# Fewer, wider loads of the factor rows on two queues, and three batches of attention in turns

## The chip, the cores and the metric

One Trainium2 chip, one core. The metric is the device time of one execution in microseconds (us); lower is better. The kernel before takes 1417.87 us (median of 3 runs, 1416.62 to 1419.35).

## What is computed

Eight batches, each of 8 heads, 576 tokens and 64 values a head, all in float32. `phi` gives each head 32 memory slots: a softmax over the tokens weighs keys and values into 32 rows each, and every token attends to these rows. The result, a row of 512 per token, goes through a "mixture of depths": a gate scores every token, the 128 best of a batch pass a two-layer network, and the others keep their row.

```python
a = softmax(phi, over tokens)            # (b, h, 576, 32)
k_m, v_m = a^T k, a^T v                  # (b, h, 32, 64)
x = softmax(q k_m^T / 8) v_m             # (b, 576, 8 * 64)
top = the 128 best of x w_gate, in each batch
out = x;  out[top] = x[top] + sigmoid(x[top] w_gate) * (relu(x[top] w1) w2)
```

## The kernel before, in words

The program is written out by hand: every engine and every DMA queue works off its instructions in the order in which the Python code issues them. Jobs are generators; `turns` (L580) steps up to `width` of them round-robin and starts a new one at least `lag` rounds after the last, `beside` (L594) puts `n` steps of another job behind each step of the first.

**Softmax and splitting (stage A, groups 0 to 7; stage B, groups 8 to 15).** A group is half a batch (4 heads). `softmax` (L156) is long work of VectorE (DVE) with ScalarE (ACT) beside it, and two groups are in turns with lag 6. Its tail `keys` (L269) transposes the weights on TensorE (PE), splits them into a high and a low part (`ahi`, `alo`, L282 to L284) and stores eight pieces to the scratch `aparts` in HBM from the queue of GpSimd (POOL, L288); another piece of `keys` forms `k_m` (L294). Beside stage A, `split_v` (L250) loads each half batch of `v` into one of two buffers (`vb`, SP queue, L254), splits it on DVE (L256, L258) and stores four copies to `vparts` from POOL (L262).

**The sums `v_m` (`values`, L303).** One call does four batches at once: `values(0)` beside stage B, `values(1)` beside the attention of batches 0 to 3 (stage C), each with two steps behind every step of the main job (L616, L633). The 576 tokens are cut into 16 chunks of T = 36. `load` (L310) brings a chunk into one of two pairs of buffers (`v_rows`, `a_rows`) by 16 transfers, all on the SP queue: eight of `a_rows` (L314; 16 partitions eight apart, pieces of 128 B, 72 KB) and then eight of `v_rows` (L320; 16 neighbouring partitions, 9216 B each, 144 KB). The loads of chunk `ch + 1` are issued as chunk `ch` begins, into the buffers that chunk `ch - 1` has left. PE then does 4 matmuls a token (L334), 2304 in all; every 16 of them are one step, so `values` has 144 steps.

**Attention and network (stage C, batches 0 to 3; stage D, batches 4 to 7).** A batch is one generator (`attention_and_ffn`, L561) of 37 steps: `centre` (L345; its first PE instruction is L348), then for three thirds of the tokens `scores` (L395) and `attend` (L435), where a third goes PE (L403), DVE (L408, L410), ACT (L412, L413), DVE (L415), PE (L443), ACT (L445), PE (L451), DVE (L454), POOL (two adds, L458), DVE (`score`, L428 to L433) and to HBM (L461); then `rank` (L465; DVE, L485, L487), `gather` (L494), `ffn1` (L514; PE L537) and `ffn2` (L544; PE L550, DVE L554, and the scatter on POOL, L556). Two batches are in turns with lag 10. All PE results pass through four PSUM banks used in turn (`bank`, L84); `xj` has two buffers, `qb`, `es` and `rd` four.

Of the kernel before, what the change touches and what calls it, by code (L numbers as in the profile page):

```python
# [9 lines left out]
F32 = mybir.dt.float32  # L10
# [5 lines left out]
AF = mybir.ActivationFunctionType  # L16
# [4 lines left out]
P = 128  # L21
# [17 lines left out]
def kernel(  # L39
# [26 lines left out]
    SET = 4  # L66
    T = 36
    scale = 1.0 / Dh ** 0.5
# [15 lines left out]
    def bank(shape, dtype=F32):  # L84
        return pss.tile(list(shape), dtype, tag="bank", name="bank")
# [11 lines left out]
    def load_q(b, j):  # L97
        qs[b, j] = step.tile([P, NPR, 2 * PT], F32, name="qb", bufs=4)
        nc.sync.dma_start(out=qs[b, j], in_=qT[b, j])
# [8 lines left out]
    kbd = [const.tile([P, NPR, 2 * M], F32, name=f"kbd{i}") for i in range(B)]  # L108
    vbd = [const.tile([P, 2, NPR * Dh], F32, name=f"vbd{i}") for i in range(2)]

# [139 lines left out]
    def split_v(b):  # L250

        for u in range(2):
            vb = io.tile([P, S * Dh * NPR // P], F32, name="vb")
            nc.sync.dma_start(out=vb, in_=v[b, u])  # L254
            hi = io.tile([P, S * Dh * NPR // P], F32, name="vhi")
            nc.vector.tensor_single_scalar(hi.bitcast(I32), vb.bitcast(I32), -4096,  # L256
                                           op=ALU.bitwise_and)
            nc.vector.tensor_sub(vb, vb, hi)  # L258
            yield
            for vp, src in enumerate((vb, hi)):  # L260
                for ap in range(2):
                    nc.gpsimd.dma_start(  # L262
                        out=vparts[b, u, ap, vp].rearrange("r s d -> (r s d)")
                                                .rearrange("(p x) -> p x", p=P), in_=src)
            yield
# [3 lines left out]
    def keys(b, g):  # L269
# [15 lines left out]
        for h in range(4):  # L285
            r, u = 2 * g + h // 2, h % 2
            for part, src in enumerate((lo, hi)):
                nc.gpsimd.dma_start(  # L288
                    out=aparts[r, b, u, part].rearrange("(c p) m -> p c m", p=PT),
                    in_=src[:, :, h * M:(h + 1) * M])  # L290
        km = bank([P, 2, 2 * M])
        for rr in range(2):
# [10 lines left out]
    def values(st):  # L303
# [6 lines left out]
        def load(ch):  # L310
            ss = slice(ch * T, (ch + 1) * T)
            for vp in range(2):
                for r in range(NPR):
                    nc.sync.dma_start(  # L314
                        out=a_rows[ch % 2][vp * 4 + r::8, :, r].bitcast(F32),
                        in_=aparts[r, b0:b0 + SET].rearrange("b u t s m -> (b u t) s m")[:, ss])
            for bb in range(SET):
                for u in range(2):
                    p0 = bb * 32 + u * 16
                    nc.sync.dma_start(  # L320
                        out=v_rows[ch % 2][p0:p0 + 16, u].rearrange("p s d -> p (s d)").bitcast(F32),
                        in_=vparts[b0 + bb, u].rearrange("t w r s d -> (t w r) (s d)")
                            [:, ch * T * Dh:(ch + 1) * T * Dh])

# [20 lines left out]
    def centre(b):  # L345
# [32 lines left out]
        for r in range(NPR):  # L378
            rows = slice(r * M, (r + 1) * M)
            nc.scalar.activation(vbd[b % 2][rows, :, r * Dh:(r + 1) * Dh], tp[rows], AF.Copy)  # L380
        means = []
# [13 lines left out]
    def scores(b, j):  # L395
# [5 lines left out]
        for c in range(2):  # L401
            for r in range(NPR):
# [7 lines left out]
        nc.vector.tensor_sub(d, heads, mx.unsqueeze(2).to_broadcast([PT, 2 * H, M]))  # L410
        e = step.tile([PT, 2 * H, M], F32, name="es", bufs=4)
        nc.scalar.activation(e, d, AF.Exp, scale=scale)  # L412
# [3 lines left out]
                                       op0=ALU.add, op1=ALU.mult)  # L416
        rd = step.tile([PT, 2, 2, NPR], F32, name="rd", bufs=4)
        rd_f = rd.rearrange("p c u r -> p (c u r)")
# [16 lines left out]
    def attend(b, j):  # L435
# [12 lines left out]
        for c in range(2):  # L448
            o = bank([PT, 2, NPR, Dh])
            for u in range(2):  # L450
                nc.tensor.matmul(out=o[:, u].rearrange("p r d -> p (r d)"), lhsT=eT[:, c, u],  # L451
                                 rhs=vbd[b % 2][:, u], start=True, stop=True)
            yield
            nc.vector.tensor_mul(x[:, c].rearrange("p (r u d) -> p u r d", u=2, d=Dh), o,  # L454
                                 rd[:, c].unsqueeze(3).to_broadcast([PT, 2, NPR, Dh]))
# [120 lines left out]
    def finish(job):  # L576
        for _ in job:
            pass
# [15 lines left out]
    def beside(main, other, n):  # L594

        for _ in main:
            for _ in range(n):
                next(other, None)
            yield
# [19 lines left out]

    work = ctx.enter_context(tc.tile_pool(name="work", bufs=2))  # L620
    one = ctx.enter_context(tc.tile_pool(name="one", bufs=1))
# [6 lines left out]
    def batch(b):  # L628
        load_q(b, 0)
        yield from attention_and_ffn(b)  # L630

    sums = values(1)
    finish(beside(turns([batch(b) for b in range(SET)], 10), sums, 2))  # L633
    finish(sums)
    finish(turns([batch(b) for b in range(SET, B)], 10))

# [33 lines left out]
```

## Time and profile before

| | |
|---|---|
| median of 3 runs | 1417.87 us |
| profiled execution: its time | 1417.34 us |
| its span (first to last instruction) | 1415.6 us |
[...]
| busy share of the span | DVE 62%, PE 51%, POOL 21%, ACT 19% |

The profile is of one execution. Times are counted from the first instruction. A share of busy time is a mean over four stages with different limits, so the stages are looked at one by one: the prediction reads windows of the span, the chain of work that ended last in a stage, the waits of an engine, and single instructions in order of time. "SPq" is the queue of SP, which issues DMAs; the share of DMA is the mean over 16 DMA engines of the time that packets took, and can pass 1 where packets overlap.

### The profile page before, as it was taken

The numbers are of one execution on the slowest core, as the hardware profiler recorded it, in microseconds if no ns is written. First come the engines' busy times: TensorE is split into PE (matmuls) and PEld (weight loads), VectorE is DVE, ScalarE is ACT, GpSimd is POOL, SyncE is SP. The second block draws the span as 40 slices with busy tenths as digits, with TensorE's granted clock in tenths as the row PEclk, the third lists the DMA queues.
The fourth block names the chain that finished last, engine by engine and source line by source line (L and its number), as shares of the span: only waits on it lengthen the run. The fifth ranks groups of instructions, "written<-read, shape, count | busy, mean of one in ns | idle before, by whom it ended". The sixth has DMA issues, their size and how long they took to land.

```text
span 1415.6 us, 16937 instructions
## 1 busy us (share of the span) xinstructions
PE 724.6 (51%) x6656; PEld 617.9 (44%) x6656; DVE 874.7 (62%) x1480; ACT 272.4 (19%) x489; POOL 297.8 (21%) x312
## 2 busy tenths in 40 slices
PE   0011111112377767842168998978545662675265
PEld 0011111112366757741157776857434542554254
DVE  8989999997857997878103234223573267346731
ACT  2212233332323332322001100002200120012000
POOL 7143211112011110111101131100431024103420
PEclk9999999999999999999999999978757755678567
DMA  6798811112999898930788888781110111010100
GB/s 195 299 360 310 336 42 42 42 42 46 122 159 144 140 152 145 154 57 17 191 129 126 142 143 138 119 151 38 56 52 19 38 56 42 22 38 30 33 19 23
DMA packets 190718, 156.05 MB, mean 110 GB/s; under 512 B 160560, under 2 KB 162608, under 8 KB 186544
## 3 DMA queue, kind: packets, MB, share of 16 engines
q1 hardware_dynamic: 171312, 94.15, 37.1%
q0 software_dynamic: 19328, 60.83, 13.4%
q8 instruction: 53, 0.87, 0.3%
q14 instruction: 25, 0.20, 0.1%
HBM read 96.21 MB, written 58.72 MB: 109 GB/s over the span
## 4 chain that ended last, share of the span: by engine, by line
DVE 34%; PE 24%; DMA 14%; SPq 12%; POOL 8%; issue 4%; ACT 3%; DVEq 0%; POOLq 0%; ACTq 0%
DMA v_rows<-vparts 9%; SPq L314 8%; PE acc L334 8%; POOL xj L458 7%; PE bank L537 5%; PE bank L550 3%; SPq L320 3%; PE bank L451 2%; PE bank L294 2%; DVE low L194 2%; DVE lo L190 2%; DVE low L193 2%; PE bank L503 2%; DVE big L191 2%; DVE lo L192 2%
## 5 line engine op out<-in xcount | busy, mean ns | idle before, releaser
L334 PE MATMUL acc<-v_rows,a_rows 32*128 32x128 f32 x4608 | 286.5, 409 | 143.0 <-DMA v_rows<-vparts 132.6
L334 PEld LDWEIGHTS acc<-v_rows,a_rows 32*128 32x128 f32 x4608 | 264.6, 319 | 172.9 <-issue 136.3
L276 PE MATMUL bank<-ident,e 128*96 128x128 f32 x96 | 24.0, 423 | 327.7 <-DVE e L245 327.7
L458 POOL TENSOR_TENSOR xj<-xj,mean 96x1024 f32<-96x1024 f32 x48 | 118.7, 2476 | 308.7 <-DVE xj L454 229.4
L276 PEld LDWEIGHTS bank<-ident,e 128*96 128x96 f32 x96 | 16.7, 193 | 330.5 <-issue 286.1
L288 POOL DMA_DIRECT2D aparts<-alo x64 | 47.1, 736 | 444.1 <-DVE alo L284 444.1
L451 PE MATMUL bank<-vbd,eT 128*96 128x256 f32 x192 | 82.4, 597 | 40.9 <-ACT eT L445 40.9
L294 PE MATMUL bank<-aS,kb 96*128 96x64 f32 x384 | 86.1, 423 | 11.7 <-ACT aS L278 11.7
L294 PEld LDWEIGHTS bank<-aS,kb 96*128 96x128 f32 x384 | 83.1, 331 | 16.5 <-ACT aS L278 15.8
L428 DVE TENSOR_TENSOR prod<-xj,wg 96x1024 f32<-96x1024 f32 x24 | 37.8, 1576 | 68.0 <-POOL xj L458 68.0
L537 PE MATMUL bank<-xeT,w_sb 128*128 128x128 f32 x512 | 73.1, 314 | 7.0 <-ACT xeT L531 7.0
L537 PEld LDWEIGHTS bank<-xeT,w_sb 128*128 128x128 f32 x512 | 71.4, 229 | 10.1 <-ACT xeT L531 10.0
L451 PEld LDWEIGHTS bank<-vbd,eT 128*96 128x96 f32 x192 | 45.8, 256 | 61.9 <-ACT eT L445 43.4
L554 DVE SCALAR_TENSOR_TENSOR ye<-bank,gr,xe 128x512 f32<-128x512 f32 x8 | 6.0, 751 | 105.0 <-PE bank L550 105.0
L408 DVE TENSOR_REDUCE smx<-bank 96x16 f32<-96x512 f32 x24 | 16.2, 673 | 87.4 <-PE bank L403 87.4
L454 DVE TENSOR_TENSOR xj<-bank,rd 96x512 f32<-96x512 f32 x48 | 31.7, 675 | 56.2 <-PE bank L451 56.2
L403 PE MATMUL bank<-kbd,qb 128*96 128x64 f32 x384 | 57.2, 332 | 8.9 <-DMA qb<-in_qT 8.9
L403 PEld LDWEIGHTS bank<-kbd,qb 128*96 128x96 f32 x384 | 56.1, 247 | 10.7 <-issue 9.1
L190 DVE SCALAR_TENSOR_TENSOR lo<-num,vh 128x576 f32<-128x576 f32 x48 | 36.2, 754 | 37.0 <-ACT vh L151 37.0
L550 PE MATMUL bank<-w_sb,hT 128*128 128x512 f32 x128 | 56.5, 594 | 0.0
L503 PE MATMUL bank<-tok,pick 96*128 96x1 f32 x96 | 21.6, 352 | 59.4 <-DVE pick L498 59.4
L194 DVE TENSOR_TENSOR low<-low,lo 128x576 f32<-128x576 f32 x64 | 48.5, 758 | 2.2
(129 smaller groups left out, 1307.7 us busy)
## 6 DMA issues: line engine op xcount, KB each, us to landing
v_rows<-vparts SPq DMA_DIRECT2D x256, 144.0 KB, 6.0
vparts<-vb POOLq DMA_DIRECT2D x32, 576.0 KB, 5.7
vparts<-vhi POOLq DMA_DIRECT2D x32, 576.0 KB, 7.5
a_rows<-aparts SPq DMA_DIRECT2D x256, 72.0 KB, 3.8
kb<-in_k SPq DMA_DIRECT2D x16, 576.0 KB, 7.8
vb<-in_v SPq DMA_DIRECT2D x16, 576.0 KB, 6.1
qb<-in_qT SPq DMA_DIRECT2D x24, 384.0 KB, 3.8
out<-xj POOLq DMA_DIRECT2D x24, 384.0 KB, 3.3
```

The lines of the kernel that those rows point to most:

```text
L190: stt(out=lo, in0=val, scalar=GRID, in1=h, op0=ALU.mult, op1=ALU.subtract)
L194: tt(out=low, in0=low, in1=lo, op=ALU.add)
L288: nc.gpsimd.dma_start(out=aparts[r, b, u, part].rearrange("(c p) m -> p c m", p=PT), in_=src[:, :, h * M:(h + 1) * M])
L294: nc.tensor.matmul(out=km[:, rr], lhsT=kb[:, c, rr * P:(rr + 1) * P], rhs=aS[:, c, rr * 2 * M:(rr + 1) * 2 * M], start=(c == 0), stop=(c = ...
L314: nc.sync.dma_start(out=a_rows[ch % 2][vp * 4 + r::8, :, r].bitcast(F32), in_=aparts[r, b0:b0 + SET].rearrange("b u t s m -> (b u t) s m") ...
L334: nc.tensor.matmul(out=accs[bb][:, :P].rearrange("p (u d) -> p u d", d=Dh), lhsT=ar[p, s].rearrange("p r m -> p (r m)"), rhs=vr[p, :, s], ...
L403: nc.tensor.matmul(out=sc[:, c, :, r], lhsT=qb[:, r, c * PT:(c + 1) * PT], rhs=kbd[b][:, r], start=True, stop=True)
L451: nc.tensor.matmul(out=o[:, u].rearrange("p r d -> p (r d)"), lhsT=eT[:, c, u], rhs=vbd[b % 2][:, u], start=True, stop=True)
L458: nc.gpsimd.tensor_add(x, x, t.unsqueeze(1).to_broadcast([PT, 2, D]))
L503: nc.tensor.matmul(out=ps[:n], lhsT=pick[:, c, :n], rhs=tok[:, c:c + 1], start=(c == 0), stop=(c == NC - 1))
L537: nc.tensor.matmul(out=ps[:, f, :n], lhsT=w1_sb[:, d, (f0 + f) * P:(f0 + f + 1) * P], rhs=xeT[:, d, :n], start=(d == 0), stop=(d == KD - 1))
L550: nc.tensor.matmul(out=ps[:n], lhsT=hT[:, f, :n], rhs=w2_sb[:, f], start=(f == 0), stop=(f == KF - 1))
```

## The change

Five things change together. (1) The chunk is 32 tokens instead of 36, so 18 chunks instead of 16. (2) `vparts` has its halves `u` outermost, so that a chunk of `v_rows` comes by two transfers of 64 partitions (every second one, 8192 B each) instead of eight. (3) `aparts` holds each part twice: POOL stores the eight pieces of a group as before, and then two new DMAs from HBM to HBM write the second copy of the low and of the high parts; the eight transfers of a chunk of `a_rows` have the same shape as before but for T, and go four each to the SP queue and to the POOL queue, behind the two of `v_rows`. (4) Three batches are in turns instead of two, in both stages, with the buffers that go with it (`vbd`, `work` three instead of two; `qb`, `es`, `rd` six instead of four). (5) In stage C one step of `values(1)` follows each step of the batches, instead of two.

```diff
--- before.py
+++ after.py
@@ -64,7 +64,7 @@
     F = w1.shape[1]
     KD, KF = D // P, F // P
     SET = 4
-    T = 36
+    T = 32
     scale = 1.0 / Dh ** 0.5
     out_flat = out.rearrange("b s d -> (b s) d")
 
@@ -95,7 +95,7 @@
         nc.sync.dma_start(out=ks[b, g], in_=k[b, g])
 
     def load_q(b, j):
-        qs[b, j] = step.tile([P, NPR, 2 * PT], F32, name="qb", bufs=4)
+        qs[b, j] = step.tile([P, NPR, 2 * PT], F32, name="qb", bufs=6)
         nc.sync.dma_start(out=qs[b, j], in_=qT[b, j])
 
     groups = [(b, g) for b in range(B) for g in range(NG)]
@@ -106,7 +106,7 @@
     make_identity(nc, ident)
 
     kbd = [const.tile([P, NPR, 2 * M], F32, name=f"kbd{i}") for i in range(B)]
-    vbd = [const.tile([P, 2, NPR * Dh], F32, name=f"vbd{i}") for i in range(2)]
+    vbd = [const.tile([P, 2, NPR * Dh], F32, name=f"vbd{i}") for i in range(3)]
 
 
     v_rows = [rows.tile([P, 2, T, Dh], F32R, name=f"v_rows{i}") for i in range(2)]
@@ -260,7 +260,7 @@
             for vp, src in enumerate((vb, hi)):
                 for ap in range(2):
                     nc.gpsimd.dma_start(
-                        out=vparts[b, u, ap, vp].rearrange("r s d -> (r s d)")
+                        out=vparts[u, b, ap, vp].rearrange("r s d -> (r s d)")
                                                 .rearrange("(p x) -> p x", p=P), in_=src)
             yield
 
@@ -286,8 +286,12 @@
             r, u = 2 * g + h // 2, h % 2
             for part, src in enumerate((lo, hi)):
                 nc.gpsimd.dma_start(
-                    out=aparts[r, b, u, part].rearrange("(c p) m -> p c m", p=PT),
+                    out=aparts[r, u, b, part, 0].rearrange("(c p) m -> p c m", p=PT),
                     in_=src[:, :, h * M:(h + 1) * M])
+        for part in range(2):
+            copies = aparts[2 * g:2 * g + 2].rearrange("r u b t w s m -> b t w (r u) (s m)")[b, part]
+            copies = copies.rearrange("w h (x y) -> w x h y", x=16)
+            nc.gpsimd.dma_start(out=copies[1], in_=copies[0])
         km = bank([P, 2, 2 * M])
         for rr in range(2):
             for c in range(NC):
@@ -309,18 +313,16 @@
 
         def load(ch):
             ss = slice(ch * T, (ch + 1) * T)
-            for vp in range(2):
-                for r in range(NPR):
-                    nc.sync.dma_start(
-                        out=a_rows[ch % 2][vp * 4 + r::8, :, r].bitcast(F32),
-                        in_=aparts[r, b0:b0 + SET].rearrange("b u t s m -> (b u t) s m")[:, ss])
-            for bb in range(SET):
+            for u in range(2):
+                nc.sync.dma_start(
+                    out=v_rows[ch % 2][u::2, u].rearrange("p s d -> p (s d)").bitcast(F32),
+                    in_=vparts[u, b0:b0 + SET].rearrange("b t w r s d -> (b t w r) (s d)")
+                        [:, ch * T * Dh:(ch + 1) * T * Dh])
+            for r in range(NPR):
                 for u in range(2):
-                    p0 = bb * 32 + u * 16
-                    nc.sync.dma_start(
-                        out=v_rows[ch % 2][p0:p0 + 16, u].rearrange("p s d -> p (s d)").bitcast(F32),
-                        in_=vparts[b0 + bb, u].rearrange("t w r s d -> (t w r) (s d)")
-                            [:, ch * T * Dh:(ch + 1) * T * Dh])
+                    (nc.sync, nc.gpsimd)[u].dma_start(
+                        out=a_rows[ch % 2][2 * r + u::8, :, r].bitcast(F32),
+                        in_=aparts[r, u, b0:b0 + SET].rearrange("b t w s m -> (b t w) s m")[:, ss])
 
         n = S // T
         load(0)
@@ -377,7 +379,7 @@
                             in_=vl.rearrange("p r m -> p (r m)"), identity=ident)
         for r in range(NPR):
             rows = slice(r * M, (r + 1) * M)
-            nc.scalar.activation(vbd[b % 2][rows, :, r * Dh:(r + 1) * Dh], tp[rows], AF.Copy)
+            nc.scalar.activation(vbd[b % 3][rows, :, r * Dh:(r + 1) * Dh], tp[rows], AF.Copy)
         means = []
         for i, src in enumerate((hi, lo)):
             yield
@@ -408,13 +410,13 @@
         nc.vector.tensor_reduce(mx, heads, axis=AX.X, op=ALU.max)
         d = step.tile([PT, 2 * H, M], F32, name="d")
         nc.vector.tensor_sub(d, heads, mx.unsqueeze(2).to_broadcast([PT, 2 * H, M]))
-        e = step.tile([PT, 2 * H, M], F32, name="es", bufs=4)
+        e = step.tile([PT, 2 * H, M], F32, name="es", bufs=6)
         nc.scalar.activation(e, d, AF.Exp, scale=scale)
         nc.scalar.activation(d, d, AF.Tanh, scale=scale / 2)
         yield
         nc.vector.scalar_tensor_tensor(out=e, in0=e, scalar=1.0, in1=d,
                                        op0=ALU.add, op1=ALU.mult)
-        rd = step.tile([PT, 2, 2, NPR], F32, name="rd", bufs=4)
+        rd = step.tile([PT, 2, 2, NPR], F32, name="rd", bufs=6)
         rd_f = rd.rearrange("p c u r -> p (c u r)")
         nc.vector.tensor_reduce(rd_f, e, axis=AX.X, op=ALU.add)
         nc.vector.tensor_scalar(out=rd_f, in0=rd_f, scalar1=float(M), scalar2=1e-9,
@@ -449,7 +451,7 @@
             o = bank([PT, 2, NPR, Dh])
             for u in range(2):
                 nc.tensor.matmul(out=o[:, u].rearrange("p r d -> p (r d)"), lhsT=eT[:, c, u],
-                                 rhs=vbd[b % 2][:, u], start=True, stop=True)
+                                 rhs=vbd[b % 3][:, u], start=True, stop=True)
             yield
             nc.vector.tensor_mul(x[:, c].rearrange("p (r u d) -> p u r d", u=2, d=Dh), o,
                                  rd[:, c].unsqueeze(3).to_broadcast([PT, 2, NPR, Dh]))
@@ -617,7 +619,7 @@
     finish(sums)
     first.close()
 
-    work = ctx.enter_context(tc.tile_pool(name="work", bufs=2))
+    work = ctx.enter_context(tc.tile_pool(name="work", bufs=3))
     one = ctx.enter_context(tc.tile_pool(name="one", bufs=1))
     step = ctx.enter_context(tc.tile_pool(name="step", bufs=2))
     w1_sb = one.tile([P, KD, F], F32, name="w1_sb")
@@ -630,9 +632,9 @@
         yield from attention_and_ffn(b)
 
     sums = values(1)
-    finish(beside(turns([batch(b) for b in range(SET)], 10), sums, 2))
+    finish(beside(turns([batch(b) for b in range(SET)], 10, 3), sums, 1))
     finish(sums)
-    finish(turns([batch(b) for b in range(SET, B)], 10))
+    finish(turns([batch(b) for b in range(SET, B)], 10, 3))
 
 
 def kernel(q, k, v, phi, moe_w_gate, moe_w1, moe_w2, moe_capacity):
@@ -661,8 +663,8 @@
         args.append(nc.dram_tensor(f"in_{name}", a.shape, mybir.dt.from_np(a.dtype),
                                    kind="ExternalInput").ap())
     out = nc.dram_tensor("out", (B, S, H * Dh), F32, kind="ExternalOutput").ap()
-    vparts = nc.dram_tensor("vparts", (B, 2, 2, 2, H // 2, S, Dh), F32, kind="Internal").ap()
-    aparts = nc.dram_tensor("aparts", (H // 2, B, 2, 2, S, phi.shape[3]), F32, kind="Internal").ap()
+    vparts = nc.dram_tensor("vparts", (2, B, 2, 2, H // 2, S, Dh), F32, kind="Internal").ap()
+    aparts = nc.dram_tensor("aparts", (H // 2, 2, B, 2, 2, S, phi.shape[3]), F32, kind="Internal").ap()
     with tile.TileContext(nc) as tc:
         tile_abc_attention__then__mixture_of_depths_kernel(tc, *args, out, vparts, aparts, int(moe_capacity))
     r = run_bass_kernel_spmd(nc, [arrays], core_ids=[0])
```

## Rows read from the trace of the kernel before

**Rows 1.** Windows (start:end, length; PE, PEld, DVE, ACT, POOL busy; PE clock; DMA share; GB/s).

```profile
213.00:320.00 107.00, 20.37 (x90) 18.68 (x90) 97.40 (x154) 35.10 (x57) 17.07 (x24) 1.00 0.16 42
363.00:613.00 250.00, 174.72 (x2367) 162.73 (x2367) 202.91 (x317) 73.11 (x116) 34.77 (x48) 1.00 0.98 146
681.00:1119.00 438.00, 308.66 (x3087) 256.49 (x3088) 150.13 (x310) 41.49 (x91) 73.57 (x44) 0.88 0.57 105
711.00:962.00 251.00, 213.02 (x2598) 181.96 (x2602) 75.31 (x155) 20.14 (x44) 35.95 (x21) 0.95 0.80 133
1142.49:1281.55 139.06, 80.41 (x394) 63.25 (x394) 75.23 (x158) 20.34 (x45) 36.96 (x22) 0.68 0.14 42
1378.00:1412.00 34.00, 19.60 (x97) 14.97 (x96) 9.12 (x21) 1.88 (x4) 3.04 (x3) 0.75 0.05 16
```

**Rows 2.** Chain of waits that ended last, by line, 363 to 613 us.

```profile
by line: DMA v_rows<-vparts 32.6%; SPq L314 28.3%; PE acc L334 14.3%; SPq L320 12.5%; PE bank L294 8.7%; issue 2.6%; PE bank L276 1.2%
```

**Rows 3.** Waits of PE, 363 to 613 us: total, times, longest.

```profile
PE acc L334 <- DMA v_rows<-vparts: 78.1, 43, 13.6
```

**Rows 4.** Waits of DVE, 363 to 613 us.

```profile
DVE lo L190 <- ACT vh L151: 20.7, 13, 6.3
DVE ahi L282 <- ACT aS L278: 16.1, 3, 9.5
```

**Rows 5.** Timeline of the SP queue, 567 to 599 us: start, us, instructions.

```profile
567.53 5.33 SPq L320 DMA_DIRECT2D v_rows<-vparts  x8
...
576.81 5.27 SPq L314 DMA_DIRECT2D a_rows<-aparts  x8
582.12 4.94 SPq L320 DMA_DIRECT2D v_rows<-vparts  x8
...
587.63 11.00 SPq L314 DMA_DIRECT2D a_rows<-aparts  x8
```

**Rows 6.** Timeline of POOL, first group of stage A.

```profile
90.07 0.73 POOL L288 DMA_DIRECT2D aparts<-ahi  x1
90.80 1.12 POOL L262 DMA_DIRECT2D vparts<-vb  x2
```

**Rows 7.** DMA issues, 213 to 320 us: count, KB each, median us to landing.

```profile
aparts<-ahi POOLq DMA_DIRECT2D x12, 72.0 KB, 4.8
```

**Rows 8.** Timeline of DVE about 109 us.

```profile
109.16 0.76 DVE L256 TENSOR_SCALAR vhi<-vb 128x1152 int32<-128x1152 int32 x1 [0.49 <-DMA vb<-in_v]
```

**Rows 9.** Timeline of POOL: first store of groups 6, 7 and 15.

```profile
319.35 0.73 POOL L288 DMA_DIRECT2D aparts<-alo  x1 [29.99 <-DVE alo L284]
...
349.82 0.73 POOL L288 DMA_DIRECT2D aparts<-alo  x1 [24.67 <-DVE alo L284]
...
675.49 0.73 POOL L288 DMA_DIRECT2D aparts<-alo  x1 [24.66 <-DVE alo L284]
```

**Rows 10.** Groups of instructions, 363 to 613 us: busy, mean ns.

```profile
L288 POOL DMA_DIRECT2D aparts<-alo x24 | 17.6, 732 | 220.4 <-DVE alo L284 220.4
```

**Rows 11.** Window of L334 alone in stage C.

```profile
711.00:962.00 251.00, 139.23 (x2289) 127.91 (x2293) 0.95 0.80 133
```

**Rows 12.** Waits of PE, 711 to 962 us.

```profile
PE acc L334 <- DMA v_rows<-vparts: 24.0, 19, 2.2
```

**Rows 13.** Timeline of PE: first sum of stage C, first steps of batches 4 and 5.

```profile
706.37 0.44 PE L334 MATMUL acc<-v_rows,a_rows 32*128 32x128 f32 x1 [27.75 <-DMA v_rows<-vparts]
...
1119.23 0.27 PE L348 MATMUL bank<-ident,v_m 128*128 128x128 f32 x1
...
1137.13 0.42 PE L348 MATMUL bank<-ident,v_m 128*128 128x128 f32 x1
```

**Rows 14.** Timeline of POOL: first adds of batches 4 and 6, last scatter.

```profile
1142.49 4.77 POOL L458 TENSOR_TENSOR xj<-xj,mean 96x1024 f32<-96x1024 f32 x2 [21.04 <-DVE xj L454]
...
1281.55 4.76 POOL L458 TENSOR_TENSOR xj<-xj,mean 96x1024 f32<-96x1024 f32 x2 [4.80 <-DVE xj L454]
...
1410.79 1.00 POOL L556 DMA_INDIRECT out<-ye,idx  x1 [21.78 <-DVE ye L554]
```

## The prediction, made before the run

> **What bounds the kernel now.** I first cut the span into windows [rows 1], because the mean shares hide four different limits, and then read in each stage which wait ends last.
>
> Where softmax runs without the sums (213 to 320 us), DVE is busy 97.4 of 107 us: it is the bound, and a group passes every 29.99 + 8 x 0.73 = 35.8 us (the idle time of POOL and its eight stores, [rows 9]). In stage B (363 to 613 us) DVE is busy only 203 of 250 us, while the DMA share is 0.98. The chain there is loads [rows 2]: landing of `v_rows` 32.6%, issuing on SP 28.3 + 12.5%. PE waits 78.1 us for `v_rows` [rows 3], and DVE pays: an ACT result arrives late 13 times, and the transposed weights 3 times, up to 9.5 us [rows 4]. A chunk holds SP for some 10 to 16 us (5.27 + 4.94, or 11.00 for `a_rows` alone, [rows 5]), and two buffers can't hide this and the landing behind the 9 us of a chunk's matmuls (139.2 us for 16, [rows 11]).
>
> In the first part of stage C (711 to 962 us) PE is busy 213 of 251 us [rows 1], 139.2 of it for the sums [rows 11]; only 24.0 us go to waits for `v_rows` [rows 12]. So here PE is near its bound, and DVE is idle for 70%. The rest of stage C and stage D have no sums: a pair of batches takes 139.06 us, from the first adds of batch 4 to those of batch 6 [rows 14], with PE busy 80.4 and DVE 75.2 [rows 1]. Nothing is full there; the chain PE, DVE, ACT, PE, DVE, POOL, DVE of two batches is the limit.
>
> **The change, part by part.** The sum is made against the profiled execution: span 1415.6 us, time 1417.34, which is 0.5 under the median of the runs.
>
> *Stage A, more on POOL.* The two new copies per group wait on POOL until the stores they read have landed. Landing takes 4.8 us in a quiet stretch [rows 7]; with two issues of some 0.7 us [rows 10] POOL is held 5 to 8 us longer per group. Behind them in its queue stand the `vparts` stores of `split_v`, which began right after the eighth store at 90.80 us [rows 6]; for their landing the next `vb` load waits, and for that DVE, which already stood 0.49 us at 109.16 [rows 8]. So the first group's delay reaches DVE nearly whole, the second's by half, and the later groups have no `v` work behind them. I take +9 us (bounds 0, if loads ahead cover it, and +16, two whole delays).
>
> *Stage B, the loads.* A chunk asks SP for 4 transfers of `a_rows` (5.27 / 8 = 0.66 each) and 2 of `v_rows` (0.5 to 0.67 as now), 4 us instead of 10 to 16, and POOL for 4 x 0.73 = 2.9 us. Is there room on the DMA engines, with a share of 0.98? In the quiet stretch the share 0.16 moves 42 GB/s, 262 per full share; in stage B 0.98 moves 146, or 149 [rows 1]. So a byte occupies the engines 1.8 times as long here. The small pieces of `a_rows` are not changed; what differs next is that each `v_rows` transfer goes to 16 neighbouring partitions, and the new ones go to 64 spread over all. I expect the occupancy to fall. [...]
>
> With the loads off the chain, DVE sets the pace again. From the first store of group 7 to that of group 15 it is now 675.49 - 349.82 = 325.7 us [rows 9]. At the pace of the quiet stretch: the first group after the change of stage, where one group runs alone, some 52 us; six at 35.8; the last 24.66 + 5.1 = 30: 297 us, a gain of 29. The bound on the other side is none. POOL's four loads may stand behind the stores and copies of a group for up to 8 x 0.73 + 4.8 + 1.4 = 12 us, but they are issued a chunk (13 us of DVE's pace) ahead, so little of it reaches PE; I keep back 5: **-24 us**.
>
> *Stage C, the sums spread over four batches.* 144 steps at one per batch step (4 x 37 = 148) fill the whole stage; now they fill the first half. From the end of the stores (675.49 + 8 x 0.73 = 681) to the first PE instruction of batch 4, 1119.23 [rows 13], stage C takes 438 us, with PE busy 308.7 [rows 1]. A step of the sums costs PE 139.2 / 144 = 0.97 us, a batch step (213.0 - 139.2) / 72 = 1.03.
>
> The order of rounds changes too. With two in turns: 10 rounds alone, 64 of two, 10 alone. With three and only four batches: 10 alone, 10 of two, 27 of three, 10 of two, and 17 in which the fourth batch is alone. In stage D an opening alone takes 1137.13 - 1119.23 = 17.9 us [rows 13], a round of two 139.06 / 37 = 3.76, an end alone 34 for 10 rounds [rows 1]: 17.9 + 64 x 3.76 + 34 = 292.5, which gives 1411.7 and matches the last scatter, 1410.79 + 1.0 [rows 14].
>
> A round of three has no row. PE's work bounds it from below, 3 x 80.4 / 74 = 3.26 us; 1.5 x 3.76 = 5.64 from above if a third batch overlaps no better. From one batch (17.9 + 34 in 20 rounds, 2.6) to two (3.76) a batch adds 1.16: I take 4.9, the line through the two rows.
>
> In stage C a round of three has 3 x (0.97 + 1.03) = 6.0 us of PE work; at the share that PE reaches now, 0.85, and somewhat better without its 24 us of waits, 0.88: 6.8 (bounds 6.2 and 8.0). Rounds of two: 3.9 of PE work over a chain of 3.76: 4.9. Alone: 22 for the opening, 57 for 17 rounds at the end (34, 17.5 for seven at 2.5, and a third of the 16.5 us of sums, which fill PE's idle time). The first sum comes 25 us after the stores now (706.37, [rows 13]); with copies (about 10) but shorter loads I take 18. So 18 + 22 + 49 + 27 x 6.8 + 49 + 57 = 379, against 438: -59. POOL's four loads stand ahead of the adds of `xj`, which are on the chain, 2.9 us a chunk; 18 chunks, half a microsecond each: +9. **-50 us** (bounds -18, with 8.0, and -84 with 6.2, no delay on POOL and half of the lone end's extra).
>
> *Stage D.* 17.9 + 37.6 + 27 x 4.9 + 37.6 + 17.5 + 34 = 276.9 against 292.5: **-16 us** (bounds +4 at 5.64, -60 at 3.26).
>
> Larger rings add no instruction, and the memsets at the start only get shorter; POOL, which does them, stands idle 30 us between two groups later [rows 9]: nothing.
>
> Sum: +9 - 24 - 50 - 16 = -81; 1417.3 - 81 = **1336 us**.
>
> **The rivals.**
>
> *The engines stay full* (0.12). If the `a_rows` pieces, which keep their 128 B, are what fills the share of 0.98, loads stay at 15.6 us a chunk. Stage B then gains nothing; stage C still does, since 250 us of loads fit into 379. 1336 + 24 = 1360. For it speaks the share; against it the 1.8 times above, which is not all explained by the pieces.
>
> *Three overlap like two* (0.15). 8.0 us a round in stage C and 5.64 in D: 27 x 1.2 + 27 x 0.74 = +52, 1388. For it: PE at 85% already; the lone end of 17 rounds is there twice.
>
> *More room than I grant* (0.22). DVE keeps its pace in B (-5), the rounds of three come near PE's work (4.2 in D: -19; 6.2 in C: -16), POOL's loads cost nothing (-9): 1287. For it: DVE and POOL are idle for half of stage D, and in stage C the sums are always ready to fill PE.
>
> *Slower: the four banks* (0.08). They stay four. A batch takes 23 of them in 37 steps (counted in the code), three batches 1.9 a round, so a bank is asked for again after two rounds in place of three; if PE then waits for the readers, the third batch overlaps with nothing. A round of three at 7.5 costs 27 x 2.6 = 70 more in each stage: 1476. It turns to slower once both stages lose 81 / 54 = 1.5 us a round on my values. Against it: a bank's reader comes one round after its writer.
>
> *POOL can't issue beside DVE* (0.03). The eight stores cost 0.73 us each while DVE is busy 81% [rows 10], so I see no such hindrance. [...]
>
> **How the numbers follow.** My forecast has 0.40. The range of 1278 to 1390 us takes in the rivals at 1287, 1360 and 1388 and leaves out the last two, 0.11, and some of the bounds' ends. A measurement can tell about 0.2% (3 us) from no change: faster 0.40 + 0.12 + 0.15 + 0.22 = 0.89, same 0.03 (the POOL rival), slower 0.08.
>
> **What would show it.** Right: stage B near 300 us between the stores of groups 7 and 15, its DMA share well under 0.9, and no `v_rows` or `a_rows` among the long waits of PE; in stage A a DVE wait for `vb` of some 8 us near 110; in stage C matmuls of L334 until the end of batch 3, DVE busy over 40%; in stage D a first long part of three batches and a last part of 50 us with one. Wrong: PE waiting for `a_rows` from POOL; PE idle before instructions that write `bank`, with the reader as releaser; rounds of three above 5.6 us in stage D; or adds of `xj` that start late behind POOL's DMAs.

## The result, and the profile after

The changed kernel takes 1302.28 us (median of 4 runs, 1301.29 to 1302.91) against 1417.91: a ratio of 0.918, 95% interval 0.917 to 0.920. 1336 was forecast, with 1278 to 1390 as its range. So the time is 34 us under the forecast, and the question is which terms of the sum were too cautious, and whether the others held for the reasons given.

The profiled execution has a span of 1300.8 us. The same marks as before cut it into stages: the first store of group 7, the first store of group 15, the first PE instruction of batch 4, the last scatter ([rows 9, 13, 14] for before). The marks of after, from the timeline of POOL (start, us, instruction), with the first group's copies on top:

```profile
89.24 0.73 POOL L288 DMA_DIRECT2D aparts<-ahi  x1
96.92 1.09 POOL L294 DMA_DIRECT2D aparts<-aparts  x2 [6.95 <-DMA aparts<-alo]
98.01 1.10 POOL L262 DMA_DIRECT2D vparts<-vb  x2
...
355.61 0.76 POOL L288 DMA_DIRECT2D aparts<-alo  x1 [19.03 <-DVE alo L284]
...
649.64 0.76 POOL L288 DMA_DIRECT2D aparts<-alo  x1 [20.81 <-DVE alo L284]
...
1296.65 1.02 POOL L558 DMA_INDIRECT out<-ye,idx  x1 [22.40 <-DVE ye L556]
```

and from that of PE (L350 is the first PE instruction of a batch, here of batches 1, 2, 4 and 5; L336 are the sums):

```profile
682.61 0.69 PE L336 MATMUL acc<-v_rows,a_rows 32*128 32x128 f32 x8 [29.84 <-DMA a_rows<-aparts]
...
704.30 0.47 PE L350 MATMUL bank<-ident,v_m 128*128 128x128 f32 x1
...
748.52 0.47 PE L350 MATMUL bank<-ident,v_m 128*128 128x128 f32 x1
...
1016.13 0.27 PE L350 MATMUL bank<-ident,v_m 128*128 128x128 f32 x1
...
1034.04 0.42 PE L350 MATMUL bank<-ident,v_m 128*128 128x128 f32 x1
```

By these marks, in us (C here runs from the first of the last eight stores, 6 us earlier than in the prediction, on both sides):

| stage | before | after | change | forecast |
|---|---|---|---|---|
| A, to the first store of group 7 | 349.8 | 355.6 | +5.8 | +9 |
| B, to that of group 15 | 325.7 | 294.0 | -31.7 | -24 |
| C, to the first step of batch 4 | 443.7 | 366.5 | -77.2 | -50 |
| D, to the last scatter | 291.6 | 280.5 | -11.1 | -16 |

Windows of after: the sums in stage B; stage C from the end of the stores; in it the first rounds of two batches, the rounds of three (from the first PE instruction of the third batch to the last of the second), the end alone; and the rounds of three in stage D, by the same marks. Columns as in [rows 1].

```profile
379.00:592.00 213.00, 162.32 (x2380) 156.31 (x2376) 194.53 (x306) 69.67 (x113) 80.38 (x122) 1.00 0.84 177
655.50:1016.10 360.60, 297.70 (x3087) 240.42 (x3088) 149.46 (x308) 42.01 (x91) 120.51 (x117) 0.88 0.54 131
704.30:748.50 44.20, 44.20 (x430) 35.26 (x426) 20.40 (x42) 7.68 (x16) 15.46 (x14) 1.00 0.59 137
748.50:922.10 173.60, 154.58 (x1602) 124.06 (x1602) 84.39 (x171) 21.07 (x45) 67.52 (x64) 0.88 0.55 124
966.30:1016.10 49.80, 35.25 (x370) 28.84 (x371) 19.02 (x40) 3.86 (x11) 8.96 (x7) 0.73 0.24 78
1063.30:1204.90 141.60, 77.46 (x397) 61.84 (x396) 89.19 (x176) 20.39 (x45) 42.15 (x24) 0.69 0.10 30
```

In stage B, DVE is now busy 194.5 of 213 us, 91%, the share that it had without any sums (97.4 of 107, [rows 1]). In stage C, PE was idle for 438 - 309 = 129 us and is now idle for 361 - 298 = 63. SP's queue in stage B (timeline) is now held by a chunk for some 4 us (the first two rows), though single groups of transfers take longer (the last):

```profile
517.74 1.13 SPq L317 DMA_DIRECT2D v_rows<-vparts  x2
518.91 2.63 SPq L323 DMA_DIRECT2D a_rows<-aparts  x4
...
526.10 9.61 SPq L323 DMA_DIRECT2D a_rows<-aparts  x4
```

DVE's waits there, against 20.7 + 16.1 in [rows 4] (that on the transposed weights, L282, is gone):

```profile
DVE lo L190 <- ACT vh L151: 9.0, 12, 0.8
DVE big L219 <- ACT low L151: 5.1, 6, 0.8
```

PE still waits for rows in stage B, 43.7 of 213 us (78.1 of 250 in [rows 3]), in 8 long pieces, and DVE's waits above do not follow them:

```profile
PE acc L336 <- DMA a_rows<-aparts: 43.7, 8, 10.3
```

### The profile page after: what moved, and what is told of

The parts are those of the page before. It is cut to its first block, busy times and chain, and to the rows that moved or that the text cites. A ratio compares the mean times of both kernels' runs of the same rounds, so it can differ in the third digit from the quotient of the medians.

```text
span 1300.8 us, 16837 instructions
## 1 busy us (share of the span) xinstructions
PE 691.2 (53%) x6656; PEld 589.1 (45%) x6656; DVE 875.1 (67%) x1480; ACT 272.0 (21%) x489; POOL 406.5 (31%) x489
## 5 line engine op out<-in xcount | busy, mean ns | idle before, releaser
L336 PE MATMUL acc<-v_rows,a_rows 32*128 32x128 f32 x4608 | 255.4, 396 | 92.4 <-DMA a_rows<-aparts 92.4
L336 PEld LDWEIGHTS acc<-v_rows,a_rows 32*128 32x128 f32 x4608 | 237.6, 305 | 123.2 <-issue 109.3
L323 POOL DMA_DIRECT2D a_rows<-aparts x144 | 90.1, 633 | 214.2 <-PE acc L336 202.6
L453 PE MATMUL bank<-vbd,eT 128*96 128x256 f32 x192 | 76.4, 551 | 14.0 <-ACT eT L447 14.0
L539 PE MATMUL bank<-xeT,w_sb 128*128 128x128 f32 x512 | 77.6, 325 | 8.5 <-ACT xeT L533 8.5
L539 PEld LDWEIGHTS bank<-xeT,w_sb 128*128 128x128 f32 x512 | 75.5, 239 | 12.0 <-ACT xeT L533 11.7
L453 PEld LDWEIGHTS bank<-vbd,eT 128*96 128x96 f32 x192 | 40.9, 232 | 31.3 <-ACT eT L447 15.1
```

Of the source, the lines that this page charges most:

```text
L323: (nc.sync, nc.gpsimd)[u].dma_start(out=a_rows[ch % 2][2 * r + u::8, :, r].bitcast(F32), in_=aparts[r, u, b0:b0 + SET].rearrange("b t w s ...
L336: nc.tensor.matmul(out=accs[bb][:, :P].rearrange("p (u d) -> p u d", d=Dh), lhsT=ar[p, s].rearrange("p r m -> p (r m)"), rhs=vr[p, :, s], ...
L539: nc.tensor.matmul(out=ps[:, f, :n], lhsT=w1_sb[:, d, (f0 + f) * P:(f0 + f + 1) * P], rhs=xeT[:, d, :n], start=(d == 0), stop=(d == KD - 1))
```

## The experiments

All ratios are to the kernel before on the same chip. The stages are those of the table above; a run whose stages are named has them from its own trace.

| kernel | us | ratio, 95% interval | A | B | C | D |
|---|---|---|---|---|---|---|
| before | 1417.91 | 1 | 349.8 | 325.7 | 443.7 | 291.6 |
| changed | 1302.28 | 0.918 (0.917 to 0.920) | 355.6 | 294.0 | 366.5 | 280.5 |
| loads_only | 1350.15 | 0.953 (0.951 to 0.955) | 354.4 | 294.1 | 404.4 | 291.5 |
| spread_only | 1367.34 | 0.965 (0.963 to 0.968) | 348.8 | 325.4 | 394.3 | 291.5 |
| loads_spread | 1338.75 | 0.945 (0.943 to 0.948) | 356.3 | 294.1 | 388.7 | 294.8 |
| loads_third | 1338.51 | 0.946 (0.943 to 0.949) | 354.1 | 294.1 | 401.1 | 280.9 |
| turns_spread_only | 1335.47 | 0.943 (0.941 to 0.945) | 348.3 | 326.7 | 372.0 | 280.1 |

### Which of the five edits pays, and where

**loads_only**: both lines of the changed kernel's main program as before, `turns([...], 10)` and `sums, 2`.

> The new loads, copies and layout alone: two batches in turns and two steps of the sums per batch step, as in the kernel before. My theory: the loads are worth what they were worth to the stages that waited for them, about -32 us in stage B, +6 in stage A, and in stage C only the 36 us in which TensorE stood waiting for rows (24.0 + 11.7), of which some 25 come back; stage D as before. About 1367 us. Rival (stage C gained through its loads, the order of the batches is worth little): stage C gains most of its 77 us here, about 1315 us.

1350 us, between the two and nearer to my theory. Stage B gets its whole gain from the loads. Stage C gains 39 us, more than my 25. Its windows, in the kernel before and here (from the first of the last stores to the first step of batch 4):

```profile
675.00:1119.00 444.00, 312.29 (x3105) 259.82 (x3105) 151.77 (x316) 42.20 (x94) 79.08 (x51) 0.88 0.57 105
```

```profile
648.50:1052.90 404.40, 297.82 (x3103) 249.11 (x3102) 151.86 (x315) 42.21 (x94) 124.66 (x125) 0.88 0.49 118
```

PE's idle time falls from 131.7 to 106.6, by the 25 us expected; PE's busy time falls by another 14.5 for the same instructions. The last section comes back to this.

**spread_only**: in the kernel before, `sums, 2` becomes `sums, 1`.

> The kernel before with one step of the sums per batch step in place of two, nothing else: old loads, two batches in turns. My theory: stage C is bound by TensorE's work while the sums run and by the chain after them, so spreading alone gains most of stage C's 77 us, some 50 to 60, even with the old loads, as a chunk then has 8 batch steps of time; stages A, B and D as before. About 1360 us. Rival (the loads' rate bounds stage C): 16 chunks at 16 us stay 251 us long, stage C gains under 15 us, above 1400 us.

1367 us; stage C gains 49 us with the old loads, just under the 50 to 60 that I expected; A, B and D gain nothing. My theory holds, the rival falls. PE's waits for rows in stage C, in the kernel before (675.5 to 1119.2 us) and here (674.2 to 1068.4); the longest is the first chunk's:

```profile
PE acc L334 <- DMA v_rows<-vparts: 54.5, 22, 27.7
```

```profile
PE acc L334 <- DMA v_rows<-vparts: 32.0, 5, 27.2
```

**loads_spread**: the changed kernel with `turns([...], 10)` twice.

> The changed kernel with two batches in turns instead of three, in both stages. My theory: only what the third batch is worth is lost: 11 us in stage D (the difference seen there) and about 15 in stage C, so about 1327 us. Rival (the third batch gives nothing, its rounds of one batch at the end eat the gain): 1302 us, or less. Rival (the third batch makes stage C): over 1350 us.

1338.8 us. The third batch is worth 36 us, not 25: 22 in stage C and 14 in D (3 of these 14 are D's 294.8 against 291.5 in the other runs of two).

**turns_spread_only**: the kernel before with T = 32, the larger rings, `turns([...], 10, 3)` twice and `sums, 1`. The shorter chunk is there to make room for the third batch's buffers (no run has three batches with T = 36), so it belongs to edit (4), which the diff does not say.

> The kernel before with its old loads (16 transfers a chunk, all on SP, 16 neighbouring partitions per transfer of v_rows), but three batches in turns and one step of the sums per batch step; chunks of 32 tokens, so that the third batch's buffers fit. My theory: stages C and D gain what they gained in the changed kernel (77 and 11 us), as 18 chunks of 16 us fit beside 360; stage B pays two more chunks of loads, +0 to +15 us; stage A as before. About 1330 us, 1325 to 1345. Rival (the new loads are needed for stage C): over 1365 us.

1335.5 us: C 372 and D 280, nearly as changed; B is untouched, so the shorter chunk by itself gains nothing there. Its windows (the sums of stage B, those of stage C):

```profile
364.00:623.00 259.00, 186.43 (x2484) 173.64 (x2484) 205.91 (x321) 72.97 (x117) 34.78 (x48) 1.00 0.90 142
705.00:1027.00 322.00, 284.50 (x3002) 229.99 (x3002) 146.69 (x297) 39.54 (x83) 74.28 (x43) 0.88 0.68 126
```

With the old loads PE is busy 284.5 of 322 us in stage C, 88%: spread out, these loads are hidden. So the 39 us of the loads in stage C and the 72 of turns and spreading are for the most part the same time: together 77.

**loads_third**: the changed kernel with `sums, 2`.

> The changed kernel with two steps of the sums per batch step instead of one: three batches in turns with the new loads, but the sums crowded into the first half of stage C. With the kernels already run this splits stage C: 445 us before, 406 with the loads, 390 with loads and spreading, 368 with all. My theory: spreading is worth as much with three batches as the 16 us with two, or more, as the crowded first half is TensorE's and the second half can't use the third batch: stage C 385 to 395 us, 1318 to 1330 in all. Rival (the third batch alone does it): stage C 370 us, 1305.

1338.5 us, stage C 401: worse than my theory and far from the rival. With the sums crowded, the third batch gives stage C 3 us (404.4 to 401.1); with the sums spread, 22 (388.7 to 366.5); and spreading gives 16 with two batches, 35 with three (401.1 to 366.5). Each needs the other. By the windows of the stage, PE is idle for 95 us here (306.0 of 401.0 busy), for 81 with the sums spread over two batches in turns (loads_spread, 307.5 of 388.7) and for 66 with both edits (300.9 of 366.5).

### The loads: form, number, queue

**v8_packed** and **v8_spread**: the two transfers of `v_rows` become eight of 16 partitions each, which differ in where they lie.

```diff
-            for u in range(2):
+            for i in range(4):
+                for u in range(2):
...
-                    out=v_rows[ch % 2][u::2, u]
+                    out=v_rows[ch % 2][32 * i + u:32 * (i + 1):2, u]   (packed; rows 16 * i:16 * (i + 1))
+                    out=v_rows[ch % 2][2 * i + u::8, u]                (spread; rows i::4)
```

> The changed kernel, but each chunk of v_rows comes by eight transfers of 16 partitions that lie within 32 neighbouring ones (every second), instead of two of 64. My theory (the form of the destination sets the rate of a packet): an 8192 B packet took 0.46 us in the changed kernel and 9216 B took 0.93 in the kernel before, where 16 partitions lay within 16; here 0.5 to 0.75 us, the DMA share in the sums of stage B rises from 0.84 to over 0.9, and the time stays within 1300 to 1312 us, as DVE and TensorE set the pace of the stages. Rival (the number of transfers was the cost): packets stay at 0.46 us and the time rises by some 36 x 6 x 0.4 = 86 us of issuing at most, over 1315 us.

> As v8_packed, with eight transfers of 16 partitions, but each lies spread over all 128 (every eighth). My theory: packets as in the changed kernel, 0.46 us, DMA share about 0.84 in the sums of stage B, 1300 to 1310 us. Rival (the number of transfers was the cost): as v8_packed, over 1315 us.

Packed: 1313.1 us (0.926, 0.922 to 0.930; runs 1310.0 to 1316.2), stage B 304.8; spread: 1306.2 (0.921, 0.918 to 0.925; runs 1304.9 to 1308.1), stage B 296.1; two transfers: 294.0. The packets' mean times in stage B (from the trace's DMA records, 8192 B each) are 0.63, 0.58 and 0.46 us, and 0.78 with the old 16 neighbours (turns_spread_only). The windows of packed and of spread, beside 0.84 and 177 GB/s above:

```profile
379.00:592.00 213.00, 151.16 (x2206) 145.38 (x2204) 184.90 (x292) 67.69 (x108) 74.76 (x114) 1.00 0.90 171
```

```profile
379.00:592.00 213.00, 159.18 (x2320) 153.15 (x2320) 192.75 (x303) 70.42 (x113) 80.33 (x122) 1.00 0.85 174
```

So both theories hold a part, and packed is a little slower than the 1312 us that I gave it. The two kernels ran on one chip and differ only in the partitions that a transfer fills, and with them the rows of `vparts` that it reads. The form is worth some 7 us (the intervals overlap, but no run of packed is as fast as the slowest of spread) and 9 in stage B, by one trace each; why packed is slower than spread, and by what the form sets a packet's time, is not shown. The number of transfers is worth 4 us at most (the intervals overlap), and a packet's time, which I took for the mark of the form, falls with it too, from 0.58 to 0.46; that was not expected. How much of 0.78 to 0.46 is which is not settled. Nor is all of stage B's gain: packed, with eight transfers of 16 partitions like the old loads, keeps 22 of the 33 us (304.8 against 326.7 in turns_spread_only and 294.0), and the old loads differ from it in the form, in the order of the transfers, in the queue and in the copies, which no run takes apart.

**one_queue**: `(nc.sync, nc.gpsimd)[u].dma_start` becomes `nc.sync.dma_start`.

> The changed kernel with all eight transfers of a_rows of a chunk on the SP queue, none on POOL. My theory: the second queue is not needed, SP is then held some 6.5 us a chunk against 20 us of a chunk in stage C and 12 in stage B; 1297 to 1306 us, and no wait of POOL for the sums. Rival (two queues are what makes the loads fast): stage B loses 10 us or more, over 1312 us.

1299.7 us (0.917, 0.914 to 0.920), stage B 294.1, stage C 364.1 against 366.5. The second queue brings nothing measurable; POOL is spared its 144 issues of 0.63 us. The transfers of `v_rows` are unchanged here, and yet their packets take 0.39 us in stage B against 0.46: a packet's time shows what else is under way, too, and not the form alone. PE waits for `a_rows` here as well, with none of them on POOL:

```profile
PE acc L336 <- DMA a_rows<-aparts: 33.6, 8, 6.7
```

**late_copies**: the loop with the two copies stands behind the `yield` that follows the matmuls of `k_m`.

> The changed kernel with the two copies of a group issued one step later in its job, so that in stage A the stores of the split v stand ahead of them on POOL. My theory: stage A's 6 us were the vparts stores held behind copies that wait for their stores; they come back, stage A ends at 349 instead of 354 us (DVE's last split), about 1297 us. Rival (the copies' traffic itself slows stage A): stage A unchanged, 1302 us.

1297.2 us (0.915, 0.911 to 0.918); the first store of group 7 at 351.1 instead of 355.6. POOL in stage A, against the rows of after above:

```profile
89.92 1.12 POOL L262 DMA_DIRECT2D vparts<-vb  x2
92.82 1.05 POOL L262 DMA_DIRECT2D vparts<-vhi  x2 [1.78 <-DMA aparts<-alo]
95.40 0.57 POOL L301 DMA_DIRECT2D aparts<-aparts  x1 [1.52 <-DMA aparts<-alo]
```

The stores of the split `v` begin at 89.92 again, and not at 98.01. The intervals of the two times overlap, so it is the trace that shows the gain. The rival falls: with its copies still made, stage A is within 1.3 us of the kernel before.

### Banks, and a version that beats both

**three_banks**: `name="pss", bufs=4` becomes 3.

> The changed kernel with three PSUM banks in turn instead of four. If four banks were near to holding three batches back, as the rival of the prediction has it, a fourth less costs rounds of three dear: stages C and D lose over 1 us in each of some 27 rounds of three, 54 us and more, over 1356 us. If a bank's reader comes well before it is asked for again (my theory), four have slack and three cost less than 30 us: 1305 to 1330 us, in all four stages.

1303.7 us (0.920, 0.917 to 0.923), no loss that can be measured. The banks have slack, more than I had thought, and the slower rival falls.

**late_one_queue**: late_copies and one_queue together.

> The changed kernel with the copies one step later and all loads of the sums on SP. Each alone gave some 3 to 5 us (1299.7 and 1297.2 us); one shortens stage A, the other stage C, so they should add: 1294 to 1296 us. If both only moved the same wait: 1297 us.

1295.1 us (0.915, 0.913 to 0.917): A 350.3, C 363.3. It has the lowest time measured here, and its interval just touches that of the changed kernel. By the ratio it can't be told from late_copies alone (0.915 both), so that the two add is shown only by the traces, one each: late_copies has A at 351.1 and C at 366.8.

**four**: the same with `turns([...], 10, 4)` twice.

> As late_one_queue, with four batches in turns in both stages, which leaves 10 rounds of one batch at the end in place of 17 and takes 67 rounds in place of 74. By rounds measured in the changed kernel (18 us for the opening, 2.9 a round of two, 4.9 to 5.4 of three, 6.5 taken for one of four, 3.4 alone at the end) stage D takes 18 + 29 + 49 + 46 + 52 + 40 + 34 = 268 us against 280, and stage C some 10 less: about 1273 us. Rival (TensorE bound in stage C, and rounds of four cost a third more than rounds of three in stage D): nothing gained, 1290 to 1300 us. Rival (the banks): slower than 1300 us.

1296.9 us (0.916, 0.914 to 0.919): D gains 3.6 us (276.5), C loses 5 (368.6). The rival holds. From the start of the fourth batch to the last matmul of the first, 22 steps of batches take 38 us (1112.57 to 1150.65), 6.9 for four steps, against 5.1 for three in the 31 steps before them:

```profile
1060.11 0.42 PE L350 MATMUL bank<-ident,v_m 128*128 128x128 f32 x1
...
1112.57 0.42 PE L350 MATMUL bank<-ident,v_m 128*128 128x128 f32 x1
...
1148.77 1.88 PE L552 MATMUL bank<-w_sb,hT 128*128 128x512 f32 x4
```

In stage D PE waits where it waited with three, for DVE in `rank` and `gather` (45.7 and 35.6 us in late_one_queue):

```profile
PE bank L505 <- DVE pick L500: 46.3, 4, 13.7
PE bank L475 <- DVE gate L435: 37.4, 4, 10.0
```

Why a fourth batch fills none of this is not shown.

## Why the prediction was right, and which terms were mis-sized

**Stage A** (+9; +5.8). The mechanism is as told: POOL waits 6.95 us for the stores, the `vparts` stores begin 7.2 us later than in [rows 6], and DVE stands for `vb` (timeline of DVE; 0.49 in [rows 8]):

```profile
112.48 0.76 DVE L256 TENSOR_SCALAR vhi<-vb 128x1152 int32<-128x1152 int32 x1 [4.53 <-DMA vb<-in_v]
```

Up to 210 us, DVE's waits for `vb` go from 7.7 us in the kernel before (first row) to 14.7 (second row), and to 9.7 in late_copies, which takes the cause away, and 4.5 of the 5.8 us with it:

```profile
DVE vhi L256 <- DMA vb<-in_v: 7.7, 4, 5.0
```

```profile
DVE vhi L256 <- DMA vb<-in_v: 14.7, 5, 5.6
```

Only the share that reaches DVE was smaller than taken.

**Stage B** (-24; -31.7). Right for its reason: loads_only has the whole gain, DVE is back at 91%. Five of its groups pass at 35.8 us, as taken, one at 36.5; the first takes 48.9 in place of 52 (stores at 355.61 and 404.47). That the new form of `v_rows` would lower the occupancy was my expectation, with no row behind it; from 379 to 592 us a share of 0.84 moves 177 GB/s, 211 per full share against 149. Nor do the pieces of `a_rows` all keep their 128 B, as I had it: in the trace's DMA records of these 213 us they have it on SP's queue alone (32768 packets), and POOL's 64 loads come as 1024 packets of 4096 B. With all eight on SP's queue the share is 0.79 for the same 177 GB/s (one_queue), so POOL's packets are not what lowers it. The step that failed is "I keep back 5" for POOL. POOL's loads do stand behind copies: its groups of instructions in stage B show 14.5 us of waits of the copies for the stores (`alo`, `ahi`). But the loads themselves wait mostly for PE to leave the buffers, 67.4 us, and only 2.8 for copies:

```profile
L323 POOL DMA_DIRECT2D a_rows<-aparts x64 | 40.1, 633 | 70.9 <-PE acc L336 67.4 <-DMA aparts<-aparts 2.8 <-issue 0.8
L294 POOL DMA_DIRECT2D aparts<-aparts x10 | 5.3, 527 | 15.4 <-DMA aparts<-alo 13.0 <-DMA aparts<-ahi 1.5 <-issue 0.8
```

A load costs 0.63 us with DVE at 91%: the rival in which POOL cannot issue beside DVE falls; that such a hindrance would cost the whole gain, as its place under "same" takes it, no run shows. One of the prediction's own signs of being wrong did come, PE waiting for `a_rows` (43.7 us), but one_queue has these waits without POOL, and the stage is as short there: they do not bound it.

**Stage C** (-50; -77). Right in sign and in mechanism (66 of the 77 us are idle time of PE), too small by 27 us, which is most of the miss. For the terms one has to know how many rounds a window holds. Each step of a batch has one step of the sums, 16 matmuls, behind it, so the count of L336 tells. The windows from batch 1 to batch 2, from there to the end of batch 1, and from there to the end of batch 2, L336 alone:

```profile
704.30:748.50 44.20, 21.91 (x340) 19.10 (x336) 1.00 0.59 137
748.50:922.10 173.60, 65.97 (x1208) 58.52 (x1208) 0.88 0.55 124
922.10:966.30 44.20, 15.35 (x340) 13.65 (x344) 0.81 0.56 126
```

That is 21, 75.5 and 21 steps, so 10.6, 25.2 and 10.6 rounds. The rounds of three came as forecast: 6.9 us against 6.8, with 6.1 us of PE's work against 6.0 and PE busy 89% against 88%. That the work fits is luck: a step of the sums took 0.87 us and not 0.97, a step of a batch 1.17 and not 1.03. The steps that failed are others. "Rounds of two: 3.9 of PE work over a chain of 3.76: 4.9": they took 4.2, as PE had no gap in the first ones (44.2 of 44.2 us), and that is 15 us in 20 rounds. The lone end, 57: its window has 49.8, two steps of batch 2 among them, some 11 us less. POOL's delay on the chain, 9: the rounds above hold what there was of it, and one_queue finds 2.4. Against these stands the first sum, for which 18 us were taken: it came 27 after the stores (682.61 against 655.5). What I had right only in part is the loads' share: I gave stage C's gain to spreading and the third batch, and loads_only shows that the loads alone would have brought half of it.

**Stage D** (-16; -11). The sum is near, but by luck. The opening is 17.9 again (1016.13 to 1034.04) and the lone end some 50 against 51.5. The rounds of three, "4.9, the line through the two rows", failed: 141.6 us for the same 75.5 steps are 5.6 a round. That is the edge of the prediction's own sign of being wrong, and next to the 5.64 of a third batch that overlaps no better than two. What paid for it are the rounds of two before them: 29.3 us (1034.04 to 1063.3), 2.8 a round, where 37.6 were taken. Those behind them took 3.8 a round, so the steps of a batch are unlike, and the average of 3.76 that the sum uses hides it.

**The rivals.** That the engines stay full falls (0.84 with more bytes, stage B gains). Three overlapping like two falls in stage C (6.9 against 8.0) and with its time of 1388 us; in stage D its price of a round is what was measured. More room than granted is right that DVE keeps its pace in B and POOL's loads cost little, but its rounds were not reached (6.2 and 4.2 wanted). The banks fall by three_banks.

## What to carry to other kernels

Two edits that cure the same idle time are not worth their sum: here the loads and the spreading bring 39 and 49 us to one stage alone, 55 together, and only with a third job in turns 77. Where one engine waits for a job's loads while the others idle, look first at how the two jobs are dealt out over the stage; the old loads were hidden as soon as a chunk had the time of eight steps. And a DMA that waits for another's landing should not stand in a queue ahead of stores that a busy engine needs: one step later it cost 1.3 us of stage A in place of 5.8.

## What the runs showed of the hardware that was not expected

The profile gives a granted PE clock of 1.00 for all of stages A and B, and for stage C up to the first change that the trace's records of the clock hold (915.8 us before, 840.0 after). The matmuls of the sums say otherwise. Groups of L334 in the kernel before, from 858 to 866, 916 to 934 and 938 to 960 us (busy us, mean ns of one):

```profile
L334 PE MATMUL acc<-v_rows,a_rows 32*128 32x128 f32 x97 | 6.1, 415 | 0.0
...
L334 PE MATMUL acc<-v_rows,a_rows 32*128 32x128 f32 x163 | 5.7, 275 | 0.0
...
L334 PE MATMUL acc<-v_rows,a_rows 32*128 32x128 f32 x173 | 12.0, 416 | 7.4 <-DMA v_rows<-vparts 4.7 <-issue 2.7
```

and the profile's clock about these times (the column before the last two):

```profile
850.00:880.00 30.00, 27.25 (x377) 23.52 (x373) 14.37 (x29) 1.37 (x3) 5.63 (x3) 1.00 0.81 131
917.00:936.00 19.00, 17.75 (x245) 13.12 (x247) 3.15 (x8) 1.20 (x2) 1.03 (x1) 1.00 0.67 108
937.00:960.00 23.00, 15.63 (x207) 14.15 (x207) 5.64 (x21) 0.97 (x4) 0.99 (x1) 0.50 0.73 151
```

A matmul takes 415 ns at the first 1.00, as at the recorded 0.50 (416), and 275 ns at the 1.00 behind the first recorded change. The ends of matmuls are modelled in the profile, but their starts say the same: four of them, one for each batch, start every 213, 112 and 213 ns in the three groups. So the level ahead of the first change is not measured, and by this pace PE ran from the first sum (366 us) until 916 us as it does at the recorded 0.50: no sum between them has the faster pace, which the profile's mean clock of 0.896 for the span hides. The pace rose while L537 (L539 after) kept PE busy without a gap, from 912 us on before and from 834 us on after. Before, the recorded fall of the clock (936.3) came 1 us behind a wait for rows of 1.25 us; after, the fall (863.9) came 0.8 us into a wait for rows of 4.22 us. The changed kernel has the faster pace from 840 us on for part of stage C; its sums there, 855 to 863 us:

```profile
L336 PE MATMUL acc<-v_rows,a_rows 32*128 32x128 f32 x160 | 5.6, 276 | 0.0
```

That is 35 ns a matmul against 63 in the first row above. My 0.97 us for a step of the sums was thus mostly a price at the slower pace, read from a row that the profile labels 0.95 [rows 11].

PE's work in stage C falls by 11 us (308.7 to 297.7); the other 66 us of the stage are idle time. Matmul by matmul, 199 of the sums' 2304 in stage C have the faster pace before and 656 after; at 28 ns each that is 13 us, so the clock can account for the 11. It does not account for loads_only, where 320 have it (3 us) and PE's work falls by 14.5, nor for loads_third, where none has it and PE's work still falls by 6 (312.3 to 306.0). So part of PE's busy time in the kernel before is something else. The sums waited for rows 22 times there, 3 times in loads_only and once in loads_third; whether these restarts make the difference is not shown.
